# Clustered attention and two feed-forward layers in one kernel: a padded tile, SyncE held to the order of emission, and half of the operand copies issued a cycle later

## The chip, the cores and the metric

One core of a Trainium2 chip. The time is that of the device in microseconds, for one execution of the whole kernel; three executions were timed before the change, and another one was recorded by the hardware profiler.

## The reference

`q`, `k`, `v` are `[2, 8, 768, 64]` (batch, heads, sequence, width) and there are 16 centroids for each head. A key is visible to a query when both fall to the same centroid:

```
q_assign = argmax(normalised q . normalised centroids)      # the same for k
mask     = q_assign[:, :, :, None] == k_assign[:, :, None, :]
scores   = where(mask, q k^T / sqrt(D), -1e9)
x        = softmax(scores) @ v                # as [1536 tokens, 512]
x        = (h * cos(h)) @ w_out,      h = x @ w_in        # 512 -> 2048 -> 512
out      = blend(h2) @ w2_out,        h2 = x @ w2_in      # relu-like, quadratic in [-1, 1]
```

## The kernel before

All matmuls of the projections run in 32 bits: an operand is kept as a rounded high part and a low part (`fp32r`), and a product is three matmuls (`mm3`, L711 to L713).

**Attention** goes over eight pairs of heads. For each pair `prep_pair` transposes q and k on TensorE, splits them into parts `th` and `tl` on GpSimd (L311, L312), computes the one-hot code of the nearest centroid (`oht`, L482), and then *stacks* for each of the two heads an operand `st0` (queries) and `st1` (keys): DMAs from SBUF to SBUF put high part, low part and one-hot rows beneath each other (L325: five copies for each head; L302: four one-hot copies for each head). `prep_pair` is a generator; every word `P` in an order string lets it do one more step.

**Cycles.** The work on the 16 heads is written out as cycles d = -1 to 15, each an order string: `S` is a score tile (four matmuls, L506 and L509, then the row maximum on VectorE, L515), `E` its exponential on ScalarE (L524, which also adds up the row into `den`), `T` and `t` a transposition of three blocks of P (L556) evacuated by ScalarE or VectorE, `V` the product P V (L570, 24 matmuls), `R` the inverses of the row sums, `X` and `Y` the scaled output and its split into parts, `W` one step of converting the feed-forward weights. Head 0 of pair i has its first score tile at the `S6` of the odd cycle d = 2i - 1, head 1 at the `S6` of the even cycle d = 2i. PRE, BEGIN, EVEN, ODD, LATE_ODD, LATE_EVEN and LAST are the strings.

`R` (`inverse`, L528) turns the sums with VectorE, has GpSimd copy four blocks into `line` (L537), sends it to DRAM (`flat`, L540) and reads it back spread over 64 partitions each (`rb`, L544, two DMAs): the read waits until the write has landed.

TensorE, ScalarE, VectorE and GpSimd run in the order of the strings (`manual_schedule`, L657). SyncE, which issues all these DMAs from one queue, isn't in that list: the framework's scheduler orders it. The queue is strictly in order at run time.

**Buffers.** `st0` and `st1` have three buffers each, two for each pair. `th` and `tl` have one buffer in the attention pool, used by pairs 0, 2, 4, 6 and 7; pairs 1, 3 and 5 use a weight buffer (L289 to L294). `nat3` and the first weight chunk share `wraw`.

**Addresses.** SBUF tiles are laid out in the order of their pools. `den` (L522), 8 floats in each of three buffers, takes 96 bytes in each partition. Everything laid out ahead of it begins at a multiple of 128 bytes: `xh` at 17408, `xl` at 41984, `w_1` at 75264, `w_0` at 95744. Everything behind it begins 96 bytes past one: `w_2` at 116064, `w_3` at 132448, `gh` at 173408, `gl` at 189792, and all tiles of the attention pool.

**Feed-forward.** For two layers, four quarters of the hidden width and three blocks of 512 tokens, `hidden` makes `h` and `output` adds up `y`: each is a block of 48 matmuls (4 x 4 x 3) of 128 x 128 by 512 columns. `hidden` multiplies `xh`, `xl` with slot `w_0` or `w_2`; `output` multiplies `gh`, `gl` with slot `w_1` or `w_3`, in turn by quarter:

```python
        t = wslot[((l * NQ + qi) * 2 + s) % len(wslot)]
```

In the first layer the weights are the stationary operand in both; in the second layer's `output` they are the moving one.

Of the kernel before, what the change touches and what calls it, by code (L numbers as in the profile page):

```python
# [33 lines left out]
def attention_moe_moe(  # L34
# [162 lines left out]
    with ExitStack() as actx:  # L197
# [78 lines left out]
                nc.scalar.activation(cn32[rows, :, r], pcv[rows, :, r], AF.Copy)  # L276

        prepped = {}

        def load_next():  # L280
            with tc.issue_after(ins(last[0])):
# [2 lines left out]
        def prep_pair(i):  # L284
# [29 lines left out]
            def stack(s):  # L314
                for h in range(2):
                    rows = slice(h * D, (h + 1) * D)
                    t = st[h][s]

                    def put(dst, n, src):

                        if i == 0 and n == h:
                            nc.gpsimd.tensor_scalar(dst, src.bitcast(F32), 1.0, 0.0,
                                                    ALU.mult, ALU.add)
                        else:
                            last[0] = nc.sync.dma_start(dst.bitcast(F32), src.bitcast(F32))  # L325
                    if s == 0:
                        put(t[0:D], 0, th[rows, 0].unsqueeze(1).to_broadcast([D, 2, S]))
                        put(t[D:P, 0], 1, tl[rows, 0])
                    else:
                        put(t[0:D, 0], 0, th[rows, 1])  # L330
                        put(t[D:P, 0], 1, th[rows, 1])
                        put(t[0:D, 1], 0, tl[rows, 1])

            for s in range(2):
                sc = D ** -0.5 if s == 0 else 1.0
# [75 lines left out]
            if i == 0:  # L411
                run_idle(NIDLE[2], ins(mm))
                for s in range(2):
                    dv, dp = dotv[s], pds[s]
                    m = mx[:, s * G // 2:(s + 1) * G // 2].rearrange("p (j h) -> p j h", h=2)
                    e = eq[:, s * G // 2:(s + 1) * G // 2].rearrange("p (j h) c -> p j h c", h=2)
                    mb = m.unsqueeze(3).to_broadcast([P, NJ, 2, C])
                    db = desc.unsqueeze(1).unsqueeze(1).to_broadcast([P, NJ, 2, C])
                    nc.vector.tensor_reduce(m, dp, AX.X, ALU.max)
                    nc.vector.tensor_tensor(e, dp, mb, ALU.is_ge)  # L420
                    nc.vector.tensor_tensor(e, e, db, ALU.mult)
                    nc.vector.tensor_reduce(m, e, AX.X, ALU.max)
                    nc.vector.tensor_tensor(dv, e, mb, ALU.is_equal)

                    po = ps_t.tile([P, HJ, P], F32, tag="t", name=f"po0_{s}")
                    for jp in range(HJ):
                        mm = nc.tensor.transpose(
                            po[:4 * C, jp],
                            dv[:, 2 * jp:2 * jp + 2].rearrange("p r h c -> p (r h c)"), ident)
                    run_idle(NIDLE[3 + s], ins(mm))  # L430
                    last_po[0] = ins(mm)
                    for h in range(2):
                        for par in range(2):
                            r0 = par * 2 * C
                            dst = st[h][s][D:D + 2 * C, 1].rearrange(
                                "c (par jp n) -> c par jp n", par=2, n=P)[:, par]
                            src = po[r0:r0 + 2 * C]
                            if s == 0:
                                nc.scalar.activation(dst, src, AF.Copy)
                            elif par:  # L440
                                nc.scalar.activation(
                                    dst, src, AF.Identity, bias=own[r0:r0 + 2 * C, 1, h:h + 1],
                                    scale=own[r0:r0 + 2 * C, 0, h:h + 1])
                            else:
                                nc.vector.tensor_scalar(
                                    dst, src, own[r0:r0 + 2 * C, 0, h:h + 1],
                                    own[r0:r0 + 2 * C, 1, h:h + 1], ALU.mult, ALU.add)
            else:
                dv = dots.rearrange("p j s h c -> p (j s h) c")
                mb = mx.unsqueeze(2).to_broadcast([P, G, C])  # L450
                dp = pd32.rearrange("p j (g c) -> p (j g) c", c=C)
                nc.vector.tensor_reduce(mx, dp, AX.X, ALU.max)
                nc.vector.tensor_tensor(eq, dp, mb, ALU.is_ge)
                yield
                nc.gpsimd.tensor_tensor(
                    eq, eq, desc.unsqueeze(1).to_broadcast([P, G, C]), ALU.mult)
                yield
                for s in range(2):
                    stack(s)
                    yield  # L460
                nc.vector.tensor_reduce(mx, eq, AX.X, ALU.max)
                yield
                nc.vector.tensor_tensor(dv, eq, mb, ALU.is_equal)
                yield
# [15 lines left out]
                nc.tensor.transpose(po[:, jp], ohv[:, jp], ident)  # L480
            oht = ap.tile([P, HJ, P], F32R, tag="oht", bufs=1, name=f"oht{i}")
            nc.scalar.activation(oht, po, AF.Identity, bias=ohbias, scale=ohscale)  # L482
            for h in range(2):
                for s in range(2):
                    for par in range(2):
                        r0 = par * 64 + s * 32 + h * C
                        dst = st[h][s][D:D + C, 1].rearrange(
                            "c (par jp n) -> c par jp n", par=2, n=P)[:, par]
                        copy(dst, oht[r0:r0 + C])
            yield  # L490

        units = [(i, h, hf) for i in range(len(pairs)) for h in range(2) for hf in range(2)]
# [25 lines left out]
        def row_exp(n):  # L518
            s, nm = ptile[n]
            d, jj = divmod(n, NJ)  # L520
            if jj == 0:
                dens[d] = xpool.tile([P, 8], F32, tag="den", bufs=3, name=f"den{d}")  # L522
            p = ap.tile([P, 2, HS], F32, tag="p", bufs=P_BUFS, name=f"p{n}")
            nc.scalar.activation(p, s[:, :, :HS], AF.Exp, bias=nm,  # L524
                                 accum_out=dens[d][:, jj:jj + 1])
            ptile[n] = p

        def inverse(d):  # L528
# [9 lines left out]
                                        1.0, 0.0, ALU.mult, ALU.add)  # L538
            flat = dram.tile([NJ, P], F32, tag="flat", name=f"flat{d}")
            nc.sync.dma_start(flat, line)  # L540
            rb[d] = xpool.tile([P, HS], F32, tag="rb", bufs=2, name=f"rb{d}")
            for hf in range(2):
                src = flat[hf * HJ:(hf + 1) * HJ].rearrange("j n -> (j n)")
# [1 line left out]

        dens = {}
        rb = {}
        pts = {}
        opsum = {}
        x32s = []  # L550
# [65 lines left out]
        def run_cycle(d, order):  # L616


            for word in order.split():
                what, arg = word[0], int(word[1:] or 0)  # L620
                n = NJ * d + arg
                if what == "S":
                    if n < NJ * NDBL:
                        scores_of(n)
                elif what == "E":
                    if n < NJ * NDBL:
                        row_exp(n)
                elif what in "Tt":
                    p_transpose(2 * d + arg // NJ, arg % NJ, what == "t")
                    next_slot()  # L630
                elif what == "P":
                    next(made, None)
                elif what == "R":
                    inverse(d)
                elif what == "V":
                    p_v(d)
                elif what == "X":
                    if opsum:
                        x_rows(min(opsum))
                elif what == "Y":  # L640
                    if x32s:
                        x_parts()
                elif what in "Ww":
                    pump(1 if d >= FIRST + (what == "w") else 0)
                elif what == "N":
                    next_slot()
            if d == 2:
                issue_chunk(0)

        PRE = "S6 N N P E6 N S7 E7 P N P S8 N P E8 N"  # L650
        BEGIN = "S3 P T0 T1 S4 E3 P T2 P P E4 P T3 S5 E5 t4 T5 P S6 T6 T7 E6 P R S7 t8 T9 E7 T10 P S8 P E8 P S9 P t11 S10 V E9 E10"
        EVEN = "P S5 T0 T1 t2 E5 P P S6 T3 T4 P E6 t5 S7 X R Y T6 P T7 E7 S8 T8 T9 E8 t10 S9 P w P E9 t11 S10 W E10 V"
        ODD = "P S5 T0 T1 t2 S6 E5 T3 X T4 t5 S7 Y E6 P T6 R E7 T7 S8 P E8 t8 T9 S9 T10 P t11 E9 W S10 V P P E10 W"
        LATE_ODD = "S5 T0 T1 t2 S6 E5 T3 R T4 t5 S7 X Y E6 T6 T7 E7 S8 E8 t8 T9 S9 T10 t11 W S10 E9 V W W E10"
        LATE_EVEN = "S5 T0 t1 t2 E5 S6 T3 T4 E6 R T5 S7 X Y E7 T6 S8 T7 W t8 S9 E8 t9 T10 E9 t11 W S10 V E10 W"
        LAST = "S5 T0 E5 t1 T2 T3 t4 R X t5 Y T6 T7 t8 T9 t10 T11 W V W W W X Y"
        with tc.manual_schedule(engines={  # L657
                mybir.EngineType.PE, mybir.EngineType.Activation,
                mybir.EngineType.DVE, mybir.EngineType.Pool}):
            for d in range(-1, NDBL):  # L660
                run_cycle(d, PRE if d < 0 else BEGIN if d == 0 else
                          {13: LATE_ODD, 14: LATE_EVEN, 15: LAST}.get(d, (EVEN, ODD)[d % 2]))
# [138 lines left out]
```

## Time and profile before

| | |
|---|---|
| three runs | 791.19, 791.89 (median), 792.48 us |
| profiled execution | 789.55 us, of which the span from first to last instruction is 787.5 us |
| busy in the span | TensorE 98%, VectorE 72%, ScalarE 46%, GpSimd 32% |
| attention | to about 254 us |
| feed-forward | from about 245 us to the end |
| mean granted TensorE clock | 0.997 of 2.4 GHz |

A row of windows gives the busy time of each engine between two moments, with its number of instructions; a matmul that began before the window is counted too. Matmuls overlap in the pipeline, so that a busy TensorE says little: the time from one group to the next says more. A row of the timeline is start, duration, engine, line, operation and tiles; in brackets stands the idle time ahead of it and what ended that. SPq is the queue of SyncE.

### The profile page before, as it was taken

To read this page: it belongs to the slowest core of one execution; us is meant where nothing else is said; L and a number is where in the kernel's file an instruction comes from. 1 tells how busy PE (TensorE), PEld (TensorE's weight loads), DVE (VectorE), ACT (ScalarE), POOL (GpSimd) and SP (SyncE) were. 2 spreads that over 40 slices of the span, in tenths; PEclk is the share of its full clock that TensorE was granted. 3 is DMA by queue.
4 is the path that set the end of the run, shared out by engine and by line. 5 is a ranking of instruction groups with operands and counts; after the bars stand their busy time and mean duration, and the time that the engine had idled before them with its cause. 6 is when DMAs were issued, how large, how long until landed. Compare 5 with 4: busy or idle time off the path is not lost.

```text
span 787.5 us, 10605 instructions
## 1 busy us (share of the span) xinstructions
PE 771.5 (98%) x3887; PEld 608.0 (77%) x3888; DVE 568.6 (72%) x822; ACT 365.1 (46%) x679; POOL 253.9 (32%) x387
## 2 busy tenths in 40 slices
PE   7989999999999999999999999999999999999998
PEld 3767787776676888888888888888888888888886
DVE  6667688785887877787788877888866787555552
ACT  6868677776584644534444333333444232212220
POOL 3546448557334522221121123423212121111110
PEclk9999999999999999999999999999999999999999
DMA  8966575675422133122131122021131111000012
GB/s 189 216 139 167 148 157 152 166 176 135 108 67 75 54 107 107 54 68 93 53 108 55 53 88 74 13 94 55 53 108 55 53 54 55 0 1 1 27 41 93
DMA packets 49139, 69.11 MB, mean 88 GB/s; under 512 B 28512, under 2 KB 33600, under 8 KB 49088
## 3 DMA queue, kind: packets, MB, share of 16 engines
q1 hardware_dynamic: 48944, 68.42, 31.2%
q8 instruction: 30, 0.49, 0.2%
q14 instruction: 21, 0.17, 0.1%
q10 hardware_dynamic: 144, 0.03, 0.0%
HBM read 46.17 MB, written 3.19 MB: 63 GB/s over the span
## 4 chain that ended last, share of the span: by engine, by line
PE 86%; ACT 5%; DMA 3%; DVE 3%; issue 2%; SPq 1%; POOL 0%; ACTq 0%; POOLq 0%; DVEq 0%
PE y L713 11%; PE h L712 11%; PE h L711 11%; PE y L712 11%; PE h L713 11%; PE y L711 11%; PE o L570 7%; PE pt L556 4%; PE s L506 3%; PE s L509 3%; ACT p L524 2%; ACT p_t L561 2%; DMA flat<-line 1%; DVE nm L515 1%; DMA st<-oht 1%
## 5 line engine op out<-in xcount | busy, mean ns | idle before, releaser
L673 POOL TENSOR_SCALAR gh<-g 128x512 fp32r<-128x512 f32 x96 | 70.6, 736 | 286.2 <-DVE g L704 168.3
L711 PE MATMUL h<-xh,w 128*128 128x512 f32 x384 | 151.0, 393 | 0.2 <-ACT p L524 0.2
L712 PE MATMUL h<-xl,w 128*128 128x512 f32 x384 | 151.1, 393 | 0.0
L713 PE MATMUL h<-xh,w 128*128 128x512 f32 x384 | 151.0, 393 | 0.0
L515 DVE TENSOR_REDUCE nm<-s 128x1 f32<-128x768 f32 x96 | 91.1, 950 | 53.9 <-PE s L509 53.0
L700 ACT ACTIVATE p<-h,ones 128x512 f32<-128x512 f32 x48 | 33.0, 688 | 137.6 <-DVE m L699 137.2
L524 ACT ACTIVATE p<-s,nm 128x768 f32<-128x768 f32 x96 | 87.4, 910 | 19.1 <-DVE nm L515 18.7
L712 PEld LDWEIGHTS h<-xl,w 128*128 128x128 f32 x384 | 72.2, 188 | 17.0 <-issue 0.6
L711 PEld LDWEIGHTS h<-xh,w 128*128 128x128 f32 x384 | 72.2, 188 | 16.7 <-issue 0.4
L713 PEld LDWEIGHTS h<-xh,w 128*128 128x128 f32 x384 | 72.2, 188 | 16.3
L677 DVE TENSOR_TENSOR gl<-g,gh 128x512 fp32r<-128x512 f32 x96 | 70.7, 737 | 18.5 <-POOL gh L673 13.1
L556 PE MATMUL pt<-ident,p 128*128 128x128 f32 x576 | 80.6, 276 | 1.0 <-DVE p_t L559 0.5
L750 DVE TENSOR_TENSOR acc<-y,acc 128x512 f32<-128x512 f32 x72 | 49.3, 686 | 38.0 <-PE y L713 38.0
L506 PE MATMUL s<-st,st 128*128 128x384 f32 x192 | 74.2, 387 | 2.1 <-ACT p L524 1.3
L713 PE MATMUL y<-gh,w 128*128 128x512 f32 x192 | 75.7, 394 | 0.0
L713 PE MATMUL y<-w,gl 128*128 128x512 f32 x192 | 75.5, 393 | 0.0
L712 PE MATMUL y<-w,gh 128*128 128x512 f32 x192 | 75.5, 393 | 0.0
L711 PE MATMUL y<-w,gh 128*128 128x512 f32 x192 | 75.4, 393 | 0.0
L712 PE MATMUL y<-gl,w 128*128 128x512 f32 x192 | 75.3, 392 | 0.0
L711 PE MATMUL y<-gh,w 128*128 128x512 f32 x192 | 75.1, 391 | 0.0
L556 PEld LDWEIGHTS pt<-ident,p 128*128 128x128 f32 x576 | 67.6, 142 | 9.3 <-ACT p L524 4.4
L561 ACT ACTIVATE p_t<-pt 128x384 f32<-128x384 f32 x127 | 58.0, 491 | 34.2 <-PE pt L556 33.8
(115 smaller groups left out, 1314.2 us busy)
## 6 DMA issues: line engine op xcount, KB each, us to landing
wraw<-in_moe_w_in_dram SPq DMA_DIRECT2D x16, 1024.0 KB
wraw<-in_moe_w_out_dram SPq DMA_DIRECT2D x16, 1024.0 KB
st<-t SPq DMA_DIRECT2D x24, 192.0 KB
st<-th SPq DMA_DIRECT2D x9, 384.0 KB
st<-tl SPq DMA_DIRECT2D x18, 192.0 KB
st<-th SPq DMA_DIRECT2D x18, 192.0 KB
nat<-in_q_dram SPq DMA_DIRECT2D x8, 384.0 KB
nat<-in_k_dram SPq DMA_DIRECT2D x8, 384.0 KB
```

What stands on the lines that cost most here:

```text
L506: nc.tensor.matmul(s[:, step, :HS], qt[:, 0, cols], kt[:, 0, kc], start=True, stop=False)
L515: nc.vector.tensor_reduce(nm, s[:, :, :HS], AX.XY, ALU.max, negate=True)
L524: nc.scalar.activation(p, s[:, :, :HS], AF.Exp, bias=nm, accum_out=dens[d][:, jj:jj + 1])
L556: nc.tensor.transpose(ps[:, jj * P:(jj + 1) * P], p[:, kt * P:(kt + 1) * P], ident)
L561: nc.scalar.activation(pt, ps, AF.Copy)
L570: nc.tensor.matmul(o[hf * D:(hf + 1) * D], prepped[i][0][:, h, kt], pts.pop((2 * d + hf, kt)), start=kt == 0, stop=kt == NJ - 1)
L673: nc.gpsimd.tensor_scalar(hi, g, 1.0, 0.0, ALU.mult, ALU.add)
L677: nc.vector.tensor_tensor(lo, g, hi.bitcast(F32), ALU.subtract)
L711: nc.tensor.matmul(o, lh, rh, start=first, stop=False)
L712: nc.tensor.matmul(o, lh, rl, start=False, stop=False)
L713: nc.tensor.matmul(o, ll, rh, start=False, stop=last)
L750: nc.vector.tensor_tensor(a, po, a, ALU.add)
```

## The change

- `den` becomes 32 floats wide: 384 bytes in three buffers, so that everything behind it moves by 288 bytes to a multiple of 128.
- SyncE joins the engines that run in the order of emission within the cycles.
- `stack_head(0)` and `one_hots(0)` put only head 0's copies at the old place; head 1's nine copies go to a word `K`, at the start of the next odd cycle.
- `inverse` only sends `flat`; the two reads into `rb` go to a word `B` (`spread`), some words later.
- Orders: `X` and `Y` of EVEN move behind `S8` and `E8`; some `P` and `W` move by a word or two; the first weight chunk is loaded after cycle 3, not 2.

```diff
+            def stack_head(h):
+                rows = slice(h * D, (h + 1) * D)
+                t = st[h][0]
+                copy(t[0:D], th[rows, 0].unsqueeze(1).to_broadcast([D, 2, S]))
+                copy(t[D:P, 0], tl[rows, 0])
+                t = st[h][1]
+                copy(t[0:D, 0], th[rows, 1])
+                copy(t[D:P, 0], th[rows, 1])
+                copy(t[0:D, 1], tl[rows, 1])
...
-                for s in range(2):
-                    stack(s)
-                    yield
+                stack_head(0)
+                yield
...
-            for h in range(2):
+            def one_hots(h):
                 for s in range(2):
                     for par in range(2):
...
+            def second_head():
+                stack_head(1)
+                one_hots(1)
+
+            one_hots(0)
+            second.append(second_head)
...
-                dens[d] = xpool.tile([P, 8], F32, tag="den", bufs=3, name=f"den{d}")
+                dens[d] = xpool.tile([P, 32], F32, tag="den", bufs=3, name=f"den{d}")
...
             nc.sync.dma_start(flat, line)
+            flats.append((d, flat))
+
+        def spread():
+            d, flat = flats.pop(0)
             rb[d] = xpool.tile([P, HS], F32, tag="rb", bufs=2, name=f"rb{d}")
...
-            if d == 2:
+            if d == 3:
                 issue_chunk(0)
...
-        EVEN = "P S5 T0 T1 t2 E5 P P S6 T3 T4 P E6 t5 S7 X R Y T6 P T7 E7 S8 T8 T9 E8 t10 S9 P w P E9 t11 S10 W E10 V"
-        ODD = "P S5 T0 T1 t2 S6 E5 T3 X T4 t5 S7 Y E6 P T6 R E7 T7 S8 P E8 t8 T9 S9 T10 P t11 E9 W S10 V P P E10 W"
+        EVEN = "P S5 T0 T1 P t2 E5 S6 T3 P T4 E6 t5 S7 R T6 P T7 E7 S8 X T8 T9 E8 Y t10 B S9 P w P E9 t11 S10 W E10 V"
+        ODD = "K S5 T0 T1 P t2 S6 E5 T3 X T4 t5 S7 Y E6 P T6 R E7 T7 S8 P E8 t8 T9 S9 T10 B P t11 E9 W S10 V P P E10 W"
...
-                mybir.EngineType.DVE, mybir.EngineType.Pool}):
+                mybir.EngineType.DVE, mybir.EngineType.Pool, mybir.EngineType.SP}):
```

BEGIN, LATE_ODD, LATE_EVEN and LAST change in the same manner: `B` in each of them, `K` in LATE_ODD.

## Rows read from the trace of the kernel before

**Rows 1.** The page: busy time by engine; the chain that ended last, by engine.

```profile
PE 771.5 (98%) x3887; PEld 608.0 (77%) x3888; DVE 568.6 (72%) x822; ACT 365.1 (46%) x679; POOL 253.9 (32%) x387
...
PE 86%; ACT 5%; DMA 3%; DVE 3%; issue 2%; SPq 1%; POOL 0%; ACTq 0%; POOLq 0%; DVEq 0%
```

**Rows 2.** Windows of attention cycles, from the start of one V to the next.

```profile
34.63:51.92 17.29, 14.56 (x102) 10.66 (x101) 8.93 (x14) 10.54 (x24) 9.36 (x15) 1.00 0.64 145
51.92:65.78 13.86, 13.75 (x94) 10.62 (x93) 10.38 (x18) 9.89 (x24) 4.13 (x11) 1.00 0.75 162
65.78:80.09 14.31, 14.31 (x102) 10.66 (x101) 8.93 (x14) 10.42 (x24) 11.55 (x18) 1.00 0.57 162
...
150.30:165.52 15.22, 14.65 (x102) 10.62 (x101) 10.82 (x18) 10.48 (x24) 12.15 (x18) 1.00 0.68 149
...
179.35:197.65 18.30, 16.39 (x103) 12.17 (x102) 10.36 (x17) 11.84 (x25) 12.87 (x20) 0.91 0.50 117
```

**Rows 3.** Timeline of TensorE: the two longest stops ahead of a score matmul.

```profile
43.79 0.45 PE L509 MATMUL s<-st,st 80*128 80x384 f32 x1 [2.73 <-DMA st<-oht]
...
187.70 0.44 PE L509 MATMUL s<-st,st 80*128 80x384 f32 x1 [1.91 <-DMA st<-oht]
```

**Rows 4.** TensorE's waits on the one-hot copies: total, times, longest.

```profile
PE s L509 <- DMA st<-oht: 5.2, 3, 2.7
```

**Rows 5.** Timeline of SyncE's queue ahead of the first stop.

```profile
22.51 11.61 SPq L325 DMA_DIRECT2D st<-t  x10
34.22 0.96 SPq L540 DMA_DIRECT2D flat<-line  x1
...
36.15 0.58 SPq L302 DMA_DIRECT2D st<-oht  x1
38.62 1.12 SPq L544 DMA_DIRECT2D rb<-flat  x2
39.80 4.96 SPq L302 DMA_DIRECT2D st<-oht  x7
```

**Rows 6.** The same queue ahead of the stop at 187.70.

```profile
170.96 0.53 SPq L136 DMA_DIRECT2D wraw<-in_moe_w_out_dram  x1
...
178.15 0.81 SPq L540 DMA_DIRECT2D flat<-line  x1
...
181.40 0.57 SPq L302 DMA_DIRECT2D st<-oht  x1
183.95 1.12 SPq L544 DMA_DIRECT2D rb<-flat  x2
185.12 4.38 SPq L302 DMA_DIRECT2D st<-oht  x7
```

**Rows 7.** Windows at and after that stop; the granted clock is third from last.

```profile
185.00:188.80 3.80, 1.89 (x13) 1.35 (x12) 1.23 (x3) 1.75 (x4) 3.63 (x5) 1.00 0.27 78
188.80:192.20 3.40, 3.40 (x17) 3.30 (x16) 2.37 (x4) 1.86 (x4) 1.94 (x4) 0.50 0.49 98
```

**Rows 8.** Windows of feed-forward blocks, TensorE alone: h by w_0, y by w_1, h by w_2, y by w_3.

```profile
374.04:384.96 10.92, 10.92 (x49) 1.00 0.27 96
...
406.82:418.04 11.22, 11.22 (x50) 1.00 0.18 71
...
440.16:451.40 11.24, 11.24 (x50) 1.00 0.27 93
...
473.84:484.76 10.92, 10.92 (x49) 1.00 0.00 0
```

**Rows 9.** Groups of instructions: L312 on GpSimd, output in shifted and in aligned tiles.

```profile
L312 POOL TENSOR_TENSOR tl<-t,th 128x384 fp32r<-128x384 f32 x16 | 16.0, 1001 | 1.4 <-DMA st<-tl 0.2
...
L312 POOL TENSOR_TENSOR t<-t,t 128x384 fp32r<-128x384 f32 x12 | 12.1, 1006 | 1.0
```

**Rows 10.** Timeline of GpSimd: pair 7's first high part, and the product with `desc`.

```profile
184.15 0.51 POOL L311 TENSOR_SCALAR th<-t 128x384 fp32r<-128x384 f32 x1 [2.02 <-DMA st<-th]
...
200.36 1.28 POOL L455 TENSOR_TENSOR eq<-eq,desc 128x384 f32<-128x384 f32 x1 [3.70 <-DVE eq L453]
```

More of the change, by code (lines that the diff above doesn't have):

```diff
@@ L278, in attention_moe_moe @@
         prepped = {}
+        second = []
         def load_next():
@@ L547, in attention_moe_moe @@
         rb = {}
+        flats = []
         pts = {}
@@ L639, in run_cycle @@
                         x_rows(min(opsum))
+                elif what == "K":
+                    if second:
+                        second.pop(0)()
+                elif what == "B":
+                    spread()
                 elif what == "Y":
@@ L646, in run_cycle @@
                     next_slot()
-            if d == 2:
+            if d == 3:
                 issue_chunk(0)
         PRE = "S6 N N P E6 N S7 E7 P N P S8 N P E8 N"
-        BEGIN = "S3 P T0 T1 S4 E3 P T2 P P E4 P T3 S5 E5 t4 T5 P S6 T6 T7 E6 P R S7 t8 T9 E7 T10 P S8 P E8 P S9 P t11 S10 V E9 E10"
-        EVEN = "P S5 T0 T1 t2 E5 P P S6 T3 T4 P E6 t5 S7 X R Y T6 P T7 E7 S8 T8 T9 E8 t10 S9 P w P E9 t11 S10 W E10 V"
-        ODD = "P S5 T0 T1 t2 S6 E5 T3 X T4 t5 S7 Y E6 P T6 R E7 T7 S8 P E8 t8 T9 S9 T10 P t11 E9 W S10 V P P E10 W"
-        LATE_ODD = "S5 T0 T1 t2 S6 E5 T3 R T4 t5 S7 X Y E6 T6 T7 E7 S8 E8 t8 T9 S9 T10 t11 W S10 E9 V W W E10"
-        LATE_EVEN = "S5 T0 t1 t2 E5 S6 T3 T4 E6 R T5 S7 X Y E7 T6 S8 T7 W t8 S9 E8 t9 T10 E9 t11 W S10 V E10 W"
-        LAST = "S5 T0 E5 t1 T2 T3 t4 R X t5 Y T6 T7 t8 T9 t10 T11 W V W W W X Y"
+        BEGIN = "S3 P T0 T1 S4 E3 P T2 P E4 P T3 S5 E5 t4 T5 P S6 T6 T7 E6 P R S7 t8 T9 E7 T10 P S8 P E8 B P S9 P t11 S10 V E9 E10"
+        EVEN = "P S5 T0 T1 P t2 E5 S6 T3 P T4 E6 t5 S7 R T6 P T7 E7 S8 X T8 T9 E8 Y t10 B S9 P w P E9 t11 S10 W E10 V"
+        ODD = "K S5 T0 T1 P t2 S6 E5 T3 X T4 t5 S7 Y E6 P T6 R E7 T7 S8 P E8 t8 T9 S9 T10 B P t11 E9 W S10 V P P E10 W"
+        LATE_ODD = "S5 T0 T1 t2 E5 S6 T3 K R T4 t5 S7 X Y E6 T6 T7 E7 S8 E8 t8 T9 S9 T10 B t11 S10 E9 V W W W E10"
+        LATE_EVEN = "S5 T0 t1 t2 E5 S6 T3 T4 E6 R T5 S7 X Y E7 T6 S8 T7 t8 W S9 E8 t9 B T10 E9 t11 W S10 V E10 W"
+        LAST = "S5 T0 E5 t1 T2 T3 X t4 R t5 Y t6 T7 t8 B T9 t10 T11 W V W W W X Y"
         with tc.manual_schedule(engines={
                 mybir.EngineType.PE, mybir.EngineType.Activation,
-                mybir.EngineType.DVE, mybir.EngineType.Pool}):
+                mybir.EngineType.DVE, mybir.EngineType.Pool, mybir.EngineType.SP}):
             for d in range(-1, NDBL):
```

## The prediction

> **What bounds the kernel now.** I read the page first. TensorE is busy 98% of the span and the chain that ended last is 86% TensorE [rows 1], so only a shorter step of TensorE, or a removed stop of it, can show. Then I cut the attention part into windows from one V to the next [rows 2]. An even cycle takes 13.86 us and an odd one 14.31 us, with TensorE busy in all or nearly all of it; of the fifteen windows, ten others lie between 11.30 and 14.38 us and repeat this. Three odd cycles stand out: 17.29 (d = 1), 15.22 (d = 9) and 18.30 us (d = 11). Third, the timeline inside them: TensorE stands still ahead of the second matmul of S6, the first that needs the one-hot rows of a new pair's head 0 [rows 3]; there are three such waits, 5.2 us together [rows 4]. Last, the feed-forward part by blocks of 48 matmuls [rows 8]. No engine makes TensorE wait there, and yet there are two speeds: 10.92 and 11.2 us. Of the twelve blocks from 374.04 to 506.94 us six take 10.92 to 10.94 and six 11.20 to 11.25, in a fixed pattern that comes back every 133 us.
>
> **SyncE's order, K and B.** SyncE's queue shows why the one-hots are late [rows 5]. Ten stack copies, for both heads, hold it from 22.51 to 34.12; `flat` goes out at 34.22; one one-hot copy goes at 36.15; then the read into `rb` stands in front, waits for `flat` to land and goes at 38.62; only at 39.80 do the other seven one-hots follow. The fourth, the last that head 0 needs, goes near 41.1, and S6 starts at 43.79. Pair 6 is the same with a weight chunk in the transfer queue besides: chunk 170.96, `flat` 178.15, one-hot 181.40, `rb` 183.95, the rest from 185.12 [rows 6], and S6 at 187.70.
>
> After the change five copies, not ten, stand ahead, and `rb` (B) comes behind head 0's four one-hots. In cycle 0 that takes 5 x 1.16 = 5.8 us of copies (11.61 for ten) and 1.1 + 2.5 us of `rb` and its wait out of the way: the fourth one-hot goes some 7 us earlier, near 34, when S6 could have gone on at 43.79 - 3.0 = 40.8. At pair 6 the gain is two stack copies' worth of queue, the 2 us wait and 1.17 us of `rb`, about 5 us: the fourth goes near 181, against a stop that began at 187.70 - 1.91 = 185.8 [rows 3]. So the three stops should go. By odd cycles of 14.31 us that is 17.29 - 14.31 = 3.0, 15.22 - 14.31 = 0.9 and 18.30 - 14.31 = 4.0 us, 7.9 us in all. The last is more than its wait, because of the clock: the window of the stop has TensorE busy for half its time at full clock, and the next 3.40 us are granted 0.50, 1.2 instead of 2.4 GHz [rows 7], which costs 3.40 / 2 = 1.7 us. With the stop that goes too. From below: if the one-hots are late by as much for a new reason, 0.
>
> K issues the other nine DMAs of each pair, 63 in seven pairs; none is added. At about 0.6 us each (4.96 for eight with gaps [rows 5]) they hold SyncE for 5.4 us at the turn from even to odd. Behind them in the queue stand the next pair's q and k, then the odd cycle's `flat`. `rb` is needed only at the next cycle's X, half a cycle and more after B, and head 1's first score tile comes a whole cycle after K, 14 us for 9 copies. The cover is that slack: I cost K and B at nothing.
>
> **What K makes late.** `th` and `tl` have one buffer and pairs 6 and 7 both use it. Already now GpSimd waits 2.02 us for pair 6's copies before it writes pair 7's `th`, at 184.15 [rows 10]. With K, head 1's five copies go only behind B of cycle 10; by the queue of [rows 6] that is near 182 to 186. Today's last copies, out before `flat` at 178.15, have landed at 184.15, 6 us behind a chunk; with 2 to 6 us to land GpSimd starts between 188 and 192, and I take 188, since the chunk is through by then. That is 4 us later than now, while cycle 11 ends 4 us earlier. Behind it stand, in GpSimd's order, pair 7's other parts, Y, `line` and the product with `desc` (L455), which runs 1.28 us at 200.36 now, when its input is there, and waits for nothing on GpSimd [rows 10]. It would run at about 200 again, but the V that ends cycle 11 then starts at 193.65, not 197.65 [rows 2], and VectorE needs the result for its `P` behind T1 of the next cycle, some 2 us after that V. VectorE would wait 0 to 2 us, with the next row maximum behind it, and 4 more if the copies land at 192. TensorE has two score buffers in hand, so I take 1.0 us lost, bounds 0 and 4.
>
> **The padded tile.** `den` itself is read by small operations off the path; its width costs nothing. What matters is that everything behind it moves to a multiple of 128 bytes. The feed-forward blocks tell where this can count [rows 8]: h by `w_0` (aligned with aligned `xh`) takes 10.92; y by `w_3` (both shifted by 96 bytes) takes 10.92; y by `w_1` (aligned with shifted `gh`) takes 11.22; h by `w_2` (shifted with aligned `xh`) 11.24. So not the shift itself costs, but unequal shifts of the two operands. After the change all are equal. Of twelve blocks, the six with unequal shifts take 11.22 + 11.20 + 11.24 + 11.20 + 11.24 + 11.25 = 67.35 against 6 x 10.925 = 65.55, 1.80 us a period, and 48 blocks are four periods: 7.2 us. Nothing else holds these blocks, since the blocks of 10.92 run today beside the same VectorE and GpSimd work.
>
> The Trainium skill speaks against this part: TensorE: Matmul & The Clock Gate, section "Step-by-step: what each phase is for", says that TensorE has two independent SBUF read ports, so that loading the next weights takes no read bandwidth from the running matmul. By it the pairing of two addresses could not matter, and this part would be worth 0 instead of 7.2 us. The rows show a dependence on the pairing whatever its cause, so the trace doesn't bear the rule out here.
>
> The same rows leave another reading: `xh`, `xl`, `w_0`, `w_1` all lie below byte 112128 of a partition, the rest above 116064, and "both in one half" is as good a rule as "equal shift"; or equal shifts may have to hold over more than 128 bytes, where the two groups still differ by 128 after the change. Under these readings the part is worth 0. I take the equal shift. Score tiles (both operands already shifted alike) gain nothing; the transposes run against an aligned identity, with no difference seen. GpSimd's L312 takes 1001 ns with a shifted output and 1006 with an aligned one [rows 9], so the elementwise engines gain nothing.
>
> **Orders and first chunk.** The moved `P`, `X`, `Y`, `W` change no amount of work, and cycles are full of TensorE: nothing, bounds -0.5 and +0.5. The first chunk goes a cycle later, 14 us, and is first read in cycle 4; 0.
>
> **Sum.** -7.9 - 7.2 + 1.0 = -14.1 us. On the profiled execution: 789.55 - 14.1 = 775.5. That execution lies 2.3 us under the median of the runs, 791.89; on that scale 777.8 us.
>
> **Rivals.** *The pairing isn't mended* (one half, longer period, or the rule above): only attention gains, 791.89 - 6.9 = 785.0. For it: [rows 8] can't tell these readings apart; against it: `w_3` with `gh` is as fast as the aligned pair, so a relation of addresses is at work, and an offset within a line is the simplest. *The stop moves on*: the one-hots of head 0, or head 1's copies, still come late, because SyncE now stands behind `flat`'s wait for `line` in order of emission, and attention gains nothing: 791.89 - 7.2 = 784.7. *Slower*: the same place in every odd cycle. If head 0's four one-hots land behind S6 in d = 3, 5, 7, 9, 11 and 13, each costs the delay and, as at 187.70, 1.7 us of halved clock. To eat 14 us, six stops must cost 2.4 us each, 0.7 of it wait; to be slower by over 0.2%, 2.6 each. It decides when the fourth one-hot, issued now some 5 us ahead of S6 in a cycle without a stop, comes 6 us later. Against it: B and five copies leave the place ahead of it. *It does nothing*: the scheduler's order was already that of emission; but [rows 5] show `rb` between the one-hots of one loop.
>
> **Chances.** Both parts as forecast 0.60; pairing not mended, attention gains 0.20; attention gains little, pairing mended 0.12; neither 0.03; slower 0.05. About 0.2% (1.6 us) is what a measurement can tell from no change: faster 0.92, same 0.03, slower 0.05. The likeliest case's own range is 775.5 (all 7.9 and 7.2, nothing lost, and half a us of orders) to 781 (4 lost at cycle 12). With the first two rivals, up to 785 and a little over: 775 to 786.
>
> **What would show it.** Right: no wait of L509 on one-hots; odd cycles all near 14.3 us; no window at 0.50 around cycle 11; `rb` behind four one-hots in the queue; GpSimd's first `th` of pair 7 later against cycle 11; all feed-forward blocks at 10.9. Wrong: blocks still at two speeds, or the whole at 11.2; a new wait of L509 on st copies; VectorE waiting on L455 in every even cycle.

## The result, and the profile after

The changed kernel takes 785.85 us (median of four runs, 785.44 to 787.21) against 792.18 us for the kernel before (four runs, 791.19 to 795.25): a ratio of 0.9917, 95% interval 0.9896 to 0.9937, 6.3 us less. 14.1 us less was forecast. The profiled execution took 786.13 us with a span of 784.2 us, 3.3 us under the span before. The executions of the kernel before scatter more than those after (35 later ones have spans of 786.0 to 795.3 us, at mean granted clocks of 0.998 down to 0.991), and the one profiled, 787.5 us at 0.997, is among the short ones.

The page after, with the same two rows:

```profile
PE 770.1 (98%) x3887; PEld 608.3 (78%) x3888; DVE 569.0 (73%) x823; ACT 363.7 (46%) x678; POOL 254.6 (32%) x387
...
PE 88%; ACT 5%; DVE 2%; DMA 2%; POOL 1%; issue 1%; SPq 1%; ACTq 0%; POOLq 0%; DVEq 0%
```

Windows of attention cycles of the changed kernel from V to V, as in [rows 2]: cycles 1, 2, 3, 9, 11, 12 and 14.

```profile
35.07:49.55 14.48, 14.48 (x103) 10.67 (x102) 8.92 (x14) 10.42 (x24) 9.35 (x15) 1.00 0.66 152
49.55:63.28 13.73, 13.67 (x94) 10.63 (x94) 10.40 (x18) 9.76 (x24) 4.23 (x11) 1.00 0.58 135
63.28:77.82 14.54, 14.54 (x102) 10.67 (x102) 8.91 (x14) 10.38 (x24) 11.48 (x18) 1.00 0.49 117
148.72:163.25 14.53, 14.53 (x102) 10.67 (x101) 9.98 (x16) 9.91 (x24) 11.56 (x17) 1.00 0.72 160
177.00:191.54 14.54, 14.54 (x103) 10.68 (x102) 9.79 (x17) 11.51 (x25) 4.88 (x7) 1.00 0.63 152
191.54:210.81 19.27, 14.83 (x88) 11.49 (x87) 11.84 (x20) 9.51 (x22) 11.99 (x21) 0.91 0.32 73
223.79:236.91 13.12, 12.92 (x85) 9.66 (x84) 10.72 (x18) 9.56 (x20) 4.71 (x10) 1.00 0.24 64
```

The three stops of [rows 2] are gone: 17.29 has become 14.48, 15.22 has become 14.53, 18.30 has become 14.54 us, 7.3 us together. Among TensorE's waits from 20 to 262 us none on a one-hot copy is left:

```profile
PE pt L579 <- DVE p_t L582: 4.3, 1, 4.3
PE s L524 <- ACT p L542: 1.1, 3, 0.8
PE pt L579 <- ACT p L542: 0.4, 1, 0.4
PE pt L579 <- ACT t L356: 0.4, 1, 0.4
PE po L490 <- ACT p L542: 0.3, 1, 0.3
PE h L739 <- ACT p L542: 0.2, 1, 0.2
```

But cycle 12, 13.78 us before, takes 19.27: 5.5 us of that are given back at one place. Before, its row was:

```profile
197.65:211.43 13.78, 13.33 (x88) 9.99 (x88) 11.45 (x20) 9.32 (x22) 3.83 (x8) 1.00 0.61 130
```

The rest is small: cycles 13 and 14 become 0.8 us shorter together (13.86 to 13.12 for cycle 14), four even cycles 0.1 each, three undisturbed odd ones are 0.2 longer each, cycle 8 is 0.5 longer. Cycle 15 is 0.4 us shorter, but that lies behind the first feed-forward matmul, and the first feed-forward block takes 17.54 us in both kernels.

Feed-forward blocks of the changed kernel, TensorE alone, in the order of [rows 8] (h by `w_0`, y by `w_1`, h by `w_2`, y by `w_3`):

```profile
372.41:383.30 10.89, 10.89 (x49) 1.00 0.28 92
405.08:416.27 11.19, 11.19 (x49) 1.00 0.28 94
438.36:449.55 11.19, 11.19 (x49) 1.00 0.25 94
471.95:482.84 10.89, 10.89 (x49) 1.00 0.00 0
```

The two speeds are still there, in the same pattern, 0.03 to 0.05 us under [rows 8] here and up to 0.09 in the second layer. Feed-forward, from its first matmul to the end, takes 540.1 us where it took 542.0. So the ledger of the span, up to the first feed-forward matmul and from there, is: stops -7.3, cycle 12 +5.5, other cycles and the start +0.4, feed-forward -1.9; -3.3 us.

The stop in cycle 12, followed through the timelines of the changed kernel. SyncE first, from the weight chunk to K (K's stack copies begin at 181.76):

```profile
167.50 0.47 SPq L136 DMA_DIRECT2D wraw<-in_moe_w_out_dram  x1
...
174.51 0.26 SPq L558 DMA_DIRECT2D flat<-line  x1
...
175.92 3.20 SPq L303 DMA_DIRECT2D st<-oht  x4
180.59 1.12 SPq L566 DMA_DIRECT2D rb<-flat  x2
181.76 0.66 SPq L303 DMA_DIRECT2D st<-th  x1
...
185.42 0.84 SPq L303 DMA_DIRECT2D st<-tl  x1
```

Then GpSimd (pair 7's first high and low part, and the product with `desc`), VectorE and TensorE:

```profile
188.59 0.51 POOL L312 TENSOR_SCALAR th<-t 128x384 fp32r<-128x384 f32 x1 [8.90 <-ACT p_t L584]
189.61 1.01 POOL L313 TENSOR_TENSOR tl<-t,th 128x384 fp32r<-128x384 f32 x1 [0.51 <-DMA st<-tl]
...
201.09 0.99 POOL L466 TENSOR_TENSOR eq<-eq,desc 128x384 f32<-128x384 f32 x1
```

```profile
196.57 0.96 DVE L533 TENSOR_REDUCE nm<-s 128x1 f32<-128x768 f32 x1 [1.24 <-PE s L527]
202.11 0.55 DVE L471 TENSOR_REDUCE mx<-eq 128x24 f32<-128x384 f32 x1 [4.58 <-POOL eq L466]
202.58 0.55 DVE L582 COPY p_t<-pt 128x384 f32<-128x384 f32 x1
```

```profile
203.18 0.55 PE L579 MATMUL pt<-ident,p 128*128 128x128 f32 x3 [4.29 <-DVE p_t L582]
```

Read upwards: TensorE waits 4.29 us for a PSUM buffer that VectorE's copy L582 has to free; that copy stands behind L471, which waits 4.58 us for GpSimd's product; GpSimd was idle for 8.90 us before it could write pair 7's `th`. The releaser named in that row, an evacuation on ScalarE, is the last one seen; the next row names the copy out of `tl`, and experiments 3, 5 and 9 show that it is these copies. After the stop the window 204.07:207.48 is granted half the clock, as in [rows 7]:

```profile
204.07:207.48 3.41, 3.41 (x16) 3.31 (x15) 2.20 (x6) 2.98 (x6) 0.83 (x4) 0.50 0.86 200
```

### The profile page after: what moved, and what is told of

It is laid out like the page before. It is cut to its first block, busy times and chain, and to the rows that moved or that the text cites. A ratio compares the mean times of both kernels' runs of the same rounds, so it can differ in the third digit from the quotient of the medians.

```text
span 784.2 us, 10590 instructions
## 1 busy us (share of the span) xinstructions
PE 770.1 (98%) x3887; PEld 608.3 (78%) x3888; DVE 569.0 (73%) x823; ACT 363.7 (46%) x678; POOL 254.6 (32%) x387
## 4 chain that ended last, share of the span: by engine, by line
PE 88%; ACT 5%; DVE 2%; DMA 2%; POOL 1%; issue 1%; SPq 1%; ACTq 0%; POOLq 0%; DVEq 0%
PE h L739 11%; PE h L741 11%; PE y L741 11%; PE h L740 11%; PE y L739 11%; PE y L740 11%; PE o L593 7%; PE pt L579 4%; PE s L524 3%; PE s L527 3%; ACT p L542 3%; ACT p_t L584 2%; PE ptq L350 1%; DVE nm L533 1%; PE dt L409 1%
```

## The experiments

Where no time over several runs is given, the kernel ran once, and its span stands against 784.2 us; the four executions of the changed kernel had spans of 783.5 to 784.4 us.

**1 and 2. Where the addresses have to agree.** Two kernels differ from the changed one only in what lies ahead of the shifted tiles.

```diff
-                dens[d] = xpool.tile([P, 32], F32, tag="den", bufs=3, name=f"den{d}")
+                dens[d] = xpool.tile([P, 32], F32, tag="den", bufs=2, name=f"den{d}")
```

> The changed kernel with den in two buffers of 128 bytes, not three: everything behind it moves back by 128 bytes and then begins at a multiple of 512, as xh, w_0 and w_1 do. Theory 1 (the two operands' addresses must agree over 256 or 512 bytes, and the change left them 128 apart): all 48 feed-forward blocks take 10.89 us, and the span falls by 24 x 0.30 = 7 us to about 777. Theory 2 (both operands in one half of the partition, whatever the offset): blocks stay at 10.89 and 11.15 to 11.20, span 784. Theory 3 (two read ports that never meet): no dependence on any address, blocks as they are.

```diff
-        rec = xpool.tile([P, 32], F32, tag="rec", name="rec")
+        rec = xpool.tile([P, 64], F32, tag="rec", name="rec")[:, :32]
```

> The changed kernel with rec 128 bytes wider: everything behind it moves on by 128 bytes, to 256 beyond a multiple of 512. If the agreement has to hold over 256 bytes, all blocks take 10.89 us and the span is near 777. If it has to hold over 512 bytes, or if the half of the partition decides, two speeds remain and the span is 784.

Spans 777.7 and 776.3 us against 784.2; in both, all blocks of the feed-forward part take 10.88 us (the first and the last, which hold other work too, left out), and feed-forward takes 532.6 us where it took 540.1: 7.5 us less. The block of y by `w_1` in the first:

```profile
404.00:414.88 10.88, 10.88 (x49) 1.00 0.29 97
```

and y by `w_1`, h by `w_2` in the second:

```profile
402.70:413.58 10.88, 10.88 (x50) 1.00 0.29 97
435.34:446.22 10.88, 10.88 (x50) 1.00 0.30 97
```

No tile crossed to another half of the partition; 128 bytes either way suffice. Agreement over 256 bytes is enough, since the second kernel's two groups differ by 256 modulo 512. The halves of the partition are out, and so is "no dependence on an address". Cycle 7 takes 15.34 us in both, 0.8 longer, for which no run gives a reason.

**3. Pair 6's second head stacked in cycle 10.**

```diff
                 stack_head(0)
+                if i == 6:
+                    stack_head(1)
                 yield
...
-                stack_head(1)
+                if i != 6:
+                    stack_head(1)
                 one_hots(1)
```

> The changed kernel with the five stack copies of pair 6's second head back behind those of its first head, in cycle 10, not at K in cycle 11 (the one-hots stay at K). If these copies hold th and tl, and so GpSimd, VectorE and TensorE in cycle 12: GpSimd writes pair 7's first th near 184, not 188.6, TensorE's stop of 4.3 us in cycle 12 falls to under 1 us, and the time falls by 4 to 5.5 us (halved clock included) to about 781 on the scale of 785.9. Rival: GpSimd is behind by its own work (Y behind E8), so that the stop stays within 1 us of 4.3 and the time is the same. Second rival: with ten copies ahead the one-hots of pair 6 come late again, as before the change: stop of 2 us at S6 of cycle 11, gain 1 to 2 us only.

786.03 us over four runs (ratio to before 0.9901, 0.9881 to 0.9921), span 783.3. Cycle 12 takes 13.67 and GpSimd writes the first part at 184.16, but cycle 11 takes 19.32: with ten copies ahead the one-hots are late again.

```profile
186.44 0.51 PE L530 MATMUL s<-st,st 80*128 80x384 f32 x1 [2.94 <-DMA st<-oht]
```

This was the second rival, though with no gain where it had 1 to 2 us. Both ends of the queue hurt, and moving pair 6's five copies only moves the stop between cycles 11 and 12.

**4. The padded tile alone, in the kernel before.**

```diff
-                dens[d] = xpool.tile([P, 8], F32, tag="den", bufs=3, name=f"den{d}")
+                dens[d] = xpool.tile([P, 32], F32, tag="den", bufs=3, name=f"den{d}")
```

> The kernel before with den padded to 32 floats and nothing else: what the addresses alone bring. By the block times of the changed kernel (10.89 against 10.92, 11.15 to 11.20 against 11.22 to 11.25), 24 x 0.03 + 24 x 0.05 = 1.9 us of feed-forward; attention as before with its three stops (7.9 us). About 790 on the scale of 792. Rival: the padded tile also moves the attention cycles (even 13.85 to 13.73, odd 14.30 to 14.54), then these numbers show here; otherwise they come from the orders.

788.45 us over ten runs (785.41 to 792.03), ratio 0.9935 (0.9908 to 0.9962). The profiled execution has the block times of the changed kernel (10.89 and 11.15 to 11.20), and feed-forward takes 540.1 us, 1.9 less. The undisturbed cycles are those of before, 13.85 and 14.29 us, so that 13.73 and 14.54 come from the orders. The stops are there, 18.58 us in cycle 1 and 19.01 in cycle 11 in this execution; its span, 788.1, is no shorter. Of the 0.65% in the runs, 1.9 us (0.24%) are shown. The rest goes in good part with the granted clock: among the runs made beside it, the spans of the kernel before go from 787.1 us at a mean clock of 0.998 to 795.0 at 0.991, those of the padded one from 783.6 at 0.998 to 790.3 at 0.994. At a like clock the padded kernel is some 2 to 4 us shorter; why its executions more often had the higher clock is left open.

**5 and 6. Pair 7 in the weight buffer, with both heads stacked at once; and both mends together.** The sixth kernel is the fifth with the wider `rec` of experiment 2.

```diff
-            if i in (1, 3, 5):
+            if i in (1, 3, 5, 7):
...
                 stack_head(0)
+                if i == 7:
+                    stack_head(1)
                 yield
...
-                stack_head(1)
+                if i != 7:
+                    stack_head(1)
                 one_hots(1)
```

> The changed kernel with pair 7's th and tl in the weight buffer that pairs 1, 3 and 5 use, and with both of its heads stacked at once in cycle 12 (the weight needs the buffer soon after); its second head's one-hots stay at K. Pair 6 keeps K. If pair 6's late copies holding the shared th and tl are the whole cause of the stop in cycle 12: GpSimd writes pair 7's first part near 179.5 instead of 188.6, cycle 12 takes 13.7 instead of 19.27 us, no halved clock in the middle, and the span falls by 5.5 us to about 778.7. Rival (GpSimd's own work, with Y moved behind E8, is too much there): at least 2 us of the stop remain. Second rival: the first weight that wants the buffer waits for pair 7's copies, VectorE behind it, and cycles 12 or 13 lose 1 to 3 us.

> The last kernel with rec 128 bytes wider, so that the feed-forward operands agree over 256 bytes: both steps that the forecast had wrong are mended. If both causes are right and independent, cycles 13.7 to 14.6 throughout, all blocks 10.88, span 776.3 - 5.2 = 771.1, about 773.5 on the clock of the runs, 1.6% under the changed kernel. If they meet (feed-forward starts earlier and waits for its weights), a span of 773 to 776 with waits of TensorE behind 240 us.

The fifth has a span of 778.3 us, 5.9 under the changed kernel. GpSimd writes pair 7's first part at 179.36 and the product waits for VectorE, not VectorE for it; cycle 12 is back at 13.67, and the mean granted clock is 1.00:

```profile
179.36 0.51 POOL L312 TENSOR_SCALAR t<-t 128x384 fp32r<-128x384 f32 x1
...
193.85 1.28 POOL L466 TENSOR_TENSOR eq<-eq,desc 128x384 f32<-128x384 f32 x1 [1.56 <-DVE eq L464]
```

```profile
176.58:191.12 14.54, 14.54 (x103) 10.67 (x102) 9.98 (x17) 11.53 (x25) 12.30 (x18) 1.00 0.67 151
191.12:204.79 13.67, 13.29 (x88) 10.00 (x88) 11.48 (x20) 9.21 (x22) 4.95 (x11) 1.00 0.67 155
```

GpSimd does the same work there, Y behind E8 included, so the rival of too much work falls; cycle 13 takes 12.99, so that no weight waits for the buffer, the second rival, either; K of pair 6 stays where it was. The sixth: span 771.1 us, 773.43 us over six runs, ratio to before 0.9767 (0.9741 to 0.9793). All blocks take 10.88 us and cycle 12 13.69, and the span is the expected one: the two causes add up. Cycle 7 alone misses the expected 13.7 to 14.6, with 15.34 us as in experiments 1 and 2.

**7. Without K**: ten copies and eight one-hots at the old place.

```diff
                 stack_head(0)
+                stack_head(1)
                 yield
...
             def second_head():
-                stack_head(1)
-                one_hots(1)
+                pass
 
             one_hots(0)
+            one_hots(1)
```

> The changed kernel without K: all ten stack copies and eight one-hots at the old place, in order of emission, B kept. If K is what took the stops of cycles 1, 9 and 11 away: a stop on one-hots returns in cycle 11 (3 us and halved clock, cycle of 19, as in the kernel with pair 6 at once), perhaps 1 us in cycles 1 and 9, and the stop in cycle 12 goes: span 783 to 784. If B and the order of emission did it: no stop on one-hots, cycle 12 mended too, span 779.

Span 799.3 us, 15 over the changed kernel, and worse than every theory. The expected stops on one-hots came, in cycles 5 (1.1 us) and 11 (3.1 us, with half the clock after it), but every odd cycle to cycle 11 is long (16.25 to 20.96 us), for another reason. VectorE's wait on `rb`, and the queue from cycle 4 on, ahead of the 18.30 us of cycle 5:

```profile
DVE rb L599 <- DMA rb<-flat: 12.9, 6, 3.2
```

```profile
85.47 10.58 SPq L303 DMA_DIRECT2D st<-t  x10
96.16 0.84 SPq L559 DMA_DIRECT2D flat<-line  x1
...
97.90 5.83 SPq L303 DMA_DIRECT2D st<-oht  x8
103.82 1.18 SPq L567 DMA_DIRECT2D rb<-flat  x2
```

In order of emission all eight one-hots stand ahead of B, the read into `rb` goes at 103.82, and X, on VectorE, waits for it with row maxima and copies behind. K keeps B early; it is not only head 0 that gains by it.

**8. Without B**: `spread()` called at the end of `inverse`.

```diff
             flats.append((d, flat))
+            spread()
...
                 elif what == "B":
-                    spread()
+                    pass
```

> The changed kernel without B: the reads into rb follow flat at once, in order of emission, so that SyncE stands behind flat's landing ahead of head 0's one-hots. If B matters: in cycle 10 flat goes at 174.5 and lands at 180.6, so the four one-hots go near 182 to 185 and S6 of cycle 11 stops 2 to 3 us; other odd cycles have slack and stay at 14.5; span 786 to 788. If K alone suffices: no new stop, span 784.

Span 788.4 us, 4.1 over the changed kernel. The queue in cycle 10, and S6 of cycle 11:

```profile
175.17 0.86 SPq L558 DMA_DIRECT2D flat<-line  x1
180.06 1.10 SPq L567 DMA_DIRECT2D rb<-flat  x2
181.28 0.52 SPq L234 DMA_DIRECT2D v<-in_v_dram  x1
181.91 2.74 SPq L303 DMA_DIRECT2D st<-oht  x4
```

```profile
185.73 0.41 PE L527 MATMUL s<-st,st 80*128 80x384 f32 x1 [1.84 <-DMA st<-oht]
```

The one-hots go at 181.91 where the changed kernel has them at 175.92, cycle 11 takes 16.61, and K, 3 us later too, makes cycle 12 21.11. The other odd cycles stay at 14.48 to 14.77. Only cycle 11 stops. From `flat` to the read into `rb` the queue takes 4.9 us ahead of it (175.17 to 180.06) and 1.2 to 3.0 us at the same place ahead of the other odd cycles. A weight chunk in front of head 0's copies is not enough as a reason: cycle 4 has one too (chunk 80.78, copies from 81.37), and cycle 5 does not stop.

**9. SyncE ordered by the scheduler**, K and B kept.

```diff
-                mybir.EngineType.DVE, mybir.EngineType.Pool, mybir.EngineType.SP}):
+                mybir.EngineType.DVE, mybir.EngineType.Pool}):
```

> The changed kernel with SyncE taken out of the list again, so that the framework's scheduler orders its queue; K, B and the orders stay. If K and B take the stops away whatever the queue's order: cycles as in the changed kernel (14.5, 13.7, one of 19), span 784 within 1 us. If the order of emission is needed: the scheduler puts a read into rb or a chunk ahead of the four one-hots again, and a stop of 1 to 3 us on one-hots appears in at least one odd cycle, span 785 to 789.

Span 782.5 us, 1.5 under the expected. No stop on one-hots; cycle 12 takes 16.31, cycles 2 and 10 take 14.3. Given K and B, the order of emission is not needed here. TensorE's stop in cycle 12 is 2.3 us, not 4.3, and the clock is not halved after it. GpSimd's row names pair 6's copies as what it waits for:

```profile
187.95 0.51 POOL L312 TENSOR_SCALAR th<-t 128x384 fp32r<-128x384 f32 x1 [7.20 <-DMA st<-th]
```

**10. A difference of 192 bytes.**

```diff
-        rec = xpool.tile([P, 32], F32, tag="rec", name="rec")
+        rec = xpool.tile([P, 48], F32, tag="rec", name="rec")[:, :32]
```

> The changed kernel with rec 64 bytes wider: the operands behind it then differ from those ahead by 192 bytes (or 64 the other way) modulo 256. If any difference within 256 bytes costs: the same 24 blocks stay at 11.15 to 11.24, span 784. If only some do (96 and 128 so far): all at 10.88, span 777.

Neither. Span 781.0. Windows of y by `w_1` in the first layer, h by `w_2` for the first and the second block of tokens, y by `w_1` in the second layer:

```profile
404.03:415.23 11.20, 11.20 (x49) 1.00 0.28 94
437.33:448.53 11.20, 11.20 (x49) 1.00 0.26 94
459.73:470.73 11.00, 11.00 (x49) 1.00 0.28 93
...
536.29:547.28 10.99, 10.99 (x49) 1.00 0.30 97
```

Some of the unequal pairs cost as much as at 96 or 128 bytes, others a third of it.

**11. Both mends, and the first P of ODD ahead of S5 again.**

```diff
-        ODD = "K S5 T0 T1 P t2 S6 E5 T3 X T4 t5 S7 Y E6 P T6 R E7 T7 S8 P E8 t8 T9 S9 T10 B P t11 E9 W S10 V P P E10 W"
+        ODD = "K P S5 T0 T1 t2 S6 E5 T3 X T4 t5 S7 Y E6 P T6 R E7 T7 S8 P E8 t8 T9 S9 T10 B P t11 E9 W S10 V P P E10 W"
```

> The kernel with both mends, and in ODD the first P back ahead of S5, as before the change. The odd cycles went from 14.30 to 14.54 with the change; if the place of this P is why, they return to 14.30 and the span falls by 6 x 0.24 = 1.4 us to 769.7, time 772.0. If not, 771.1 and 773.4.

771.27 us over six runs (770.96 to 771.40), ratio to before 0.9731 (0.9699 to 0.9763); span 769.1. The odd cycles are at 14.30 again, cycle 7 among them:

```profile
62.36:76.66 14.30, 14.30 (x102) 10.65 (x101) 8.92 (x14) 10.41 (x24) 11.46 (x18) 1.00 0.52 123
```

This version is the shortest of all that were run: 14.6 us under the changed kernel.

## Why the prediction was right and where it was wrong

6.3 us came where 14.1 were forecast. The step that failed is the pairing of addresses, 7.2 us of the sum; a second term, the loss behind K, was mis-sized. That 785.85 still lies in the range of 775 to 786 is luck: the ledger of the span closes at -3.3 us, and the other 3 us come from the profiled execution of the kernel before lying 2.6 us under its median and the one after 0.3 over; where the longer executions of the kernel before lose that time, no trace shows. Nor does 785.85 confirm the rival that says 785.0: that has 6.9 us from attention, and the first feed-forward matmul came only 1.4 us sooner.

**The stops on one-hots: right.** -7.9 us was forecast, -7.3 came in cycles 1, 9 and 11. The difference is the 0.2 us by which an odd cycle grew with the place of one P (experiment 11), against which "the moved words change nothing" was off. The reasons hold in part: with K left out the one-hots are late in cycles 5 and 11, with B left out in cycle 11 (experiments 7 and 8). Neither brings the waits of cycles 1 and 9 on one-hots back, and no run leaves both out, so that for these two it is not shown which of the parts is needed. What was not forecast is the second use of K, which keeps `rb` early; and that the order of emission, counted as part of the cause, is not needed (experiment 9).

**"After the change all are equal": wrong, and the largest miss.** The rows showed that unequal shifts cost 0.30 us a block against equal ones; the step that failed is the modulus. Equal over 128 bytes was taken as equal, but after the change the two groups were still 128 apart, and the two speeds stayed. The term of 7.2 us came to 1.9, because both kinds of block became a little shorter (in the mean 0.03 us where the shifts agree and 0.06 where they don't), for a reason that no run gives. The forecast had this as a reading that the rows couldn't exclude, and gave it with the others 0.20. 128 bytes more or less are worth 6.5 to 7.9 us of span and 7.5 us of feed-forward (experiments 1 and 2), so that the size was right for operands that do agree. The Trainium skill's rule of two independent read ports (TensorE: Matmul & The Clock Gate, "Step-by-step: what each phase is for") would give no such dependence. The runs show one for these operands, and decide: 11.19 us a block became 10.88 by moving addresses alone.

**"I take 1.0 us lost" behind K: the right mechanism, mis-sized.** Place and chain are as forecast: GpSimd starts at 188.59 (188 was forecast), the product runs at 201.09 (about 200), VectorE waits for it in cycle 12. That the moments agree is luck in part: the whole cycle came 2.3 us sooner than on the forecast's clock, so that from the V that begins cycle 10 (165.52 before, 163.25 after) GpSimd's start is 25.3 us away where 22.5 was forecast. The cost is 5.5 us, beyond the upper bound of 4. Three things were missed. The V that ends cycle 11 was put at 193.65 by taking off cycle 11's stop alone; with the stops of cycles 1 and 9 gone too it starts at 191.54, and VectorE comes to the product 2 us earlier. And TensorE's two score buffers cover almost nothing: it stops for 4.29 of VectorE's 4.58 us, because the copy that frees a PSUM buffer for the next transposes stands behind the wait as well. And the clock, granted at 0.50 for 3.41 us after the stop, was priced at 1.7 us for the old stop [rows 7] and left out for the new one. Of the 5.5 us, TensorE is idle for 4.0 more than before in the cycle and busy for 1.5 more (14.83 against 13.33). Experiment 5 takes the shared buffer away and gets 5.9 us of span.

**"Nothing, bounds -0.5 and +0.5" for the orders:** -0.8 us in cycles 13 and 14, -0.4 in four even cycles, +0.6 in three odd ones, +0.5 in cycle 8. The sum, about 0, is within the bounds, and by parts that cancel; why cycles 13 and 14 are shorter was not tried apart.

With the pairing as it turned out and the stop at its measured size, the forecast's own sum gives -7.9 - 1.9 + 5.5 = -4.3 us; the spans say -3.3, the medians of the runs -6.3. Two numbers of the forecast do not come out of their own terms. The 4.96 us read as eight copies are seven in [rows 5], and the nine of K, put at 5.4 us, take 7.6 in cycle 11 of the changed kernel (181.76 to 189.37). And on the scale of the runs the lower end of the range is 791.89 - 7.9 - 7.2 - 0.5 = 776.3, not 775.5.

## What to carry to other kernels

When two operands' addresses matter, ask over how many bytes they have to agree, and price each modulus that the rows leave open: here one kernel with a tile 128 bytes wider would have told. When a copy is issued later to clear a queue, look for the single-buffered tile that it reads: the next writer waits, and with it all that stands behind that writer in its engine's order. And when several stops go at once, put all later moments on the new clock before judging whether a late result is still early enough.

## What the runs showed of the hardware

In the feed-forward blocks a matmul of 512 columns in `fp32r` goes every 10.88 / 48 = 0.227 us when its stationary and moving operands begin at the same place modulo 256 bytes (differences of 0 and, modulo 512, 256 were run; a block took up to 10.94 us in the kernel before), and every 11.20 / 48 = 0.233 us at differences of 96 or 128 bytes (11.15 to 11.25 us a block). At 192 bytes y by `w_1` takes 11.20 us a block with `gh` moving and 10.99 with `gh` stationary. h by `w_2`, whose weights are stationary throughout, has both values: in the first layer 11.20 for the first block of tokens and 11.00 for the others, in the second layer 10.99 to 11.00 for all, for which no run gives a reason. The mechanism stays open. The 32-bit transposes of P showed no such dependence: from start to start the median is 0.109 us before and after and in experiments 1, 2 and 10.
